# Later loads of the output weights, and two steps' attention weights transposed by DMA, in a thresholded attention with a SwiGLU layer behind it

## The chip, the cores and the metric

The kernel runs on one core of a Trainium2 chip. The metric is the device time of one execution in microseconds (us), here the median of 7 executions.

## The reference

The attention has 8 batches of 8 heads, 576 positions and a head width of 64. A row's weights are cut off below its maximum less `tau` (0.02). Its output, 4608 tokens of width 512, goes through an RMS norm and a gated layer of width 1536.

```python
scores = scale * np.matmul(q, k.transpose(0, 1, 3, 2))
thresh = np.max(scores, axis=-1, keepdims=True) - tau
scores = np.where(scores >= thresh, scores, -1000000000.0)
attn = np.exp(scores - np.max(scores, axis=-1, keepdims=True))
attn = attn / (np.sum(attn, axis=-1, keepdims=True) + 1e-09)
x = heads_joined(np.matmul(attn, v))               # 4608 x 512
xn = x / np.sqrt(np.mean(x * x, axis=-1, keepdims=True) + 1e-06) * rms_g
g = xn @ w_gate
out = (g * (1.0 / (1.0 + np.exp(-g))) * (xn @ w_val)) @ w_out
```

## The kernel before, in words

**Steps.** The work is cut into 144 score steps, counted from 0 in the code. A step is one pair of heads for one chunk of 128 query rows: 36 chunks by 4 head pairs. Each step goes through the same stations:

1. PE multiplies q by k in 32-bit floats into `s_ps` (line 697). I call this a burst, S. Until step 32 a burst is one step; after that, steps run together and are cut into bursts of 1024 columns (`CHOP`, line 1193).
2. DVE reads `s_ps`, scales it into one of three `ssb` buffers and finds the row extremes `mx` (line 730).
3. POOL makes the threshold `nth` from `mx` (line 771, some 0.2 us).
4. ACT applies the threshold, once for each head (line 782), and then the exponential into one of three 16-bit buffers `wsb` (line 789).
5. The weights of the step, 128 by 1152, are transposed into one of six `wt` buffers. There are two ways (lines 830 to 853). Either PE transposes nine blocks of 128 by 128 into PSUM (line 834; I call this T) and DVE copies them out in two pieces (line 843). Or SP issues one DMA transpose (line 849).
6. For two steps at a time PE multiplies `wt` by the values `va` (lines 870 and 875; I call this A), and DVE divides by the row sums (lines 892 and 893).

After four steps a chunk is complete: it is normed (ACT line 910, POOL lines 913 to 918) and transposed into `xnT`. Two or four chunks form a group of the gated layer. For each of its 12 blocks PE runs G (line 976, gate) and V (line 981, value), ACT a tanh (line 990), DVE two products (lines 993 and 998). Then O (line 1047, and line 1022 for the last group) multiplies by the output weights `wo`.

**Weights.** `w_gate` and `w_val` are loaded in twelve transfers through three staging buffers by SP (line 1125), and POOL scales and rounds them (line 1133). `wo` is loaded by four transfers of 384 KB that POOL issues (line 1145); no O can start before all four have landed.

**What sets the order.** All instructions are recorded as `Op` objects with an engine, an assumed cost, a priority and dependencies. `order_ops` (line 56) then plays a schedule with these assumed costs and writes each engine's instruction order out; the engines run in that fixed order. Where several operations of an engine could start at the same planned moment, the one with the smallest priority goes first. The priority is the step number plus an offset from the table `RANK` (line 26), looked up by the function that recorded the operation:

```python
        if o.prio >= 8.0 and o.eng != "SP":
            path = o.fn.__qualname__.split(".")
            o.prio += RANK.get(o.eng, {}).get((path[-3] if path[-3].startswith((
                "emit", "load", "setup", "transposed", "round")) else "main") + "/" + path[-1], 0.0)
```

A gated operation also waits for the burst of a certain step. The loads of `wo` are gated in this way (lines 1144 to 1147):

```python
        o = add("POOL", COST["pool_dma"], W_FROM + W_STEP * n + j + WO_AT, [], lambda o, j=j: nc.gpsimd.dma_start(
            out=wo[:, 3 * j:3 * j + 3], in_=wo_src[:, 3 * j:3 * j + 3]), dma=DMA_NS['wo'], bulk=True)
        wo_ld.append(gated(o, W_FROM + W_STEP * n + j + WO_AT))
```

With `W_FROM` 2.0, `W_STEP` 0.4 and n at 24 this is step 11 for the first load and step 14 for the last. The way of a step's transpose is chosen by this line:

```python
        if s < N_PE or s < N_ALT and s % 2:
```

Before, `N_PE` and `N_ALT` are both 16, so steps 0 to 15 go through PE and DVE and the other 128 through DMA.

Of the kernel before, what the change touches and what calls it, by code (L numbers as in the profile page):

```python
# [12 lines left out]

LAT = dict(PE=200.0, ACT=130.0, DVE=175.0, POOL=20.0, SP=0.0)
SELF = dict(PE=0.0, ACT=125.0, DVE=178.0, POOL=0.0, SP=0.0)
COST = dict(
# [7 lines left out]
SWITCH = 125.0  # L24

RANK = dict(
    ACT={"emit_ffn/ev": 450, "emit_ffn/store": 110, "emit_ffn/tanh": -300, "emit_k_tail/ev": -210, "emit_q_tail/ev": -80, "emit_qk/ev": 370,
        "emit_softmax/ex2": 60, "emit_softmax/prelu": 220, "emit_x/sq": -330},
    DVE={"emit_blocks/turn_k": 120, "emit_blocks/turn_kt": 288, "emit_blocks/turn_q": 293, "emit_burst/ttr": -57.4, "emit_ffn/ev": 320,
        "emit_ffn/gate": 60, "emit_ffn/silu": -59, "emit_k_tail/ev": 80, "emit_qk/ev": -20, "emit_softmax/ev": 320, "emit_x/ev": 50},  # L30
    PE={"emit_av/fn": -370, "emit_burst/fn": 16, "emit_ffn/gmm": 20, "emit_ffn/omm": 23, "emit_ffn/vmm": -40, "emit_k_tail/tr": 210, "emit_q_tail/tr":
        -160, "emit_qk/tr": 60, "emit_softmax/tr": -40, "emit_x/trp": 20},
    POOL={"emit_block_loads/swap": 40, "emit_softmax/nthr": -240, "emit_x/mean": -150, "emit_x/norm": -10, "round_/<lambda>": 130, "main/<lambda>":
        700, "main/cast": -280},
)


# [18 lines left out]
def order_ops(ops, ring_sizes):  # L56
# [26 lines left out]
    while len(out) < len(ops):  # L83
        best = None
        for e, lst in pending.items():
# [5 lines left out]
            for i in lst:  # L91
                o = ops[i]
                t = max(t0, ready_at[i])
                if o.ring is not None:
# [3 lines left out]
                    t = max(t, sorted(free)[o.nring - 1][0])  # L98
                other = e == "PE" and o.mode != mode
                t = max(t, o.release)  # L100
# [11 lines left out]
        cost = o.cost  # L112
        if e == "PE":
            if o.mode != mode:
# [35 lines left out]
def kernel(  # L150
# [98 lines left out]
    def gated(o, step):  # L249
        gates.append((o, step))  # L250
        return o

    def add(eng, cost, prio, deps, fn, **kw):
        o = Op(eng, cost, prio, deps, fn, **kw)
        ops.append(o)
        return o
# [30 lines left out]
    def setup():  # L287
        o_id = add("POOL", 2000.0, -100, [], lambda o: make_identity(nc, id32))

        def zero(o):  # L290
            nc.vector.memset(zcol, 0.0)
            nc.vector.memset(xn[0], 0.0)

        o_z = add("DVE", 350.0, -200, [], zero)

        def warm(o):

            for _ in range(WARM):
                nc.tensor.matmul(s_ps[0][:, 0:512], xn[0][:, 0:128], xn[0], start=True, stop=True)

        o_w = add("PE", WARM * 380.0, -200, [o_z], warm)

        def consts(o):
            nc.vector.tensor_copy(out=id16, in_=id32)
            nc.vector.memset(mhalf, -0.5)

        def vconst(o):
            for i in range(2):
                nc.vector.memset(va[i][:, :, :, D:D + 1], 1.0)
                nc.vector.memset(va[i][64:128, :, 8], 0.0)  # L310
                nc.vector.memset(va[i][0:64, :, 9], 0.0)

        o_c = add("DVE", 300.0, -100, [o_id, o_z], consts)
        o_v = add("DVE", 2000.0, -90, [], vconst)
        o_g = add("SP", 350.0, -0.5, [], lambda o: nc.sync.dma_start(
            out=rmsg, in_=moe_rms_g.rearrange("(c p) -> p c", p=128)), dma=100.0)
        return o_id, o_c, o_v, o_g
# [4 lines left out]
    def emit_qk(b, p, prio):  # L322
# [13 lines left out]
        def tr(o):  # L336
            for j in (1, 0):
                for c in range(4):
                    for r, rs in enumerate(HALF):
# [4 lines left out]

        t = gated(add("PE", COST["tr_qk"], -500.0, los + [o_id] + last_s.get(("k", b - 2, p), []), tr, ring="R",
                      nring=2, mode=1), prio)
        done = []
        for r, rs in enumerate(HALF):
            def ev(o, r=r, rs=rs):
                src = ring[t.slot[r]].rearrange("p (j c n) -> p j c n", j=2, n=64)  # L350
                if EVAC[r] == "ACT":
                    nc.scalar.copy(out=dst[:, :, :, rs], in_=src)
                else:
                    nc.vector.tensor_copy(out=dst[:, :, :, rs], in_=src)

            done.append(add(EVAC[r], COST["evac_qk" if EVAC[r] == "DVE" else "evac_qk_act"], prio, [t], ev, frees=(t, r)))
        for j in range(2):
# [7 lines left out]
    def emit_block_loads(b, g, base, prio):  # L365

        done = {}
        for j, src in ((1, k), (0, q)):
# [14 lines left out]
            for h in range(2):  # L383
# [4 lines left out]
                for dst, at in moves:  # L388
                    def swap(o, dst=dst, at=at):
                        nc.gpsimd.tensor_copy(out=dst, in_=at)  # L390

                    last = [add("POOL", COST["swap"], prio + SWAP_AT, last, swap)]
                spare_use.append(last[0])
# [28 lines left out]
    def emit_first():  # L422
# [13 lines left out]
        def load_k(p, prio):  # L436
# [6 lines left out]

            return add("SP" if p else "ACT", COST["sp_qk"], prio, before, load, dma=DMA_NS["qk"], bulk=True)

# [10 lines left out]
        def transposed(load, srcs, dsts, prio, engines):  # L456
# [9 lines left out]
            for e, (eng, lo, hi) in enumerate(engines):  # L466
                def ev(o, eng=eng, lo=lo, hi=hi):
                    copy = nc.scalar.copy if eng == "ACT" else nc.vector.tensor_copy
                    for i, m, dst in dsts:
                        if lo <= i < hi:  # L470
                            rs = slice(dst.base_partition(), dst.base_partition() + dst.shape[0])
                            copy(out=dst, in_=ring[t.slot[0]][rs, n * i:n * (i + m)].rearrange("p (a n) -> p a n", n=n))
# [13 lines left out]
        def emit_k(p, load, prio):  # L486
            nat = qkn[p % NQK]
            t, k_ready[p] = transposed(load, [pair(nat[:, 1, c]) for c in range(4)],
                                       [(0, 2, qkT[0][p][:, 0, 0:2]), (2, 2, qkT[0][p][:, 0, 2:4])], prio,
                                       [("ACT" if p in (1, 2) else "DVE", 0, 2), ("ACT", 2, 4)])  # L490
            tr_of[1].append(t)
# [84 lines left out]
    def emit_v(b, prio):  # L576
# [6 lines left out]
        def round_(dst, src):  # L583
            return lambda o: nc.gpsimd.tensor_scalar(out=dst, in0=src, scalar1=1.0, scalar2=1.0,
                                                     op0=ALU.mult, op1=ALU.mult)

        def free(p):
            return [o_v] + last_av.get((b - 2, p), [])

        for p in range(NP):  # L590
# [12 lines left out]
            if b >= BLOCKED and p == 0:  # L603
                lo = []
                for i in range(2 * V_PARTS):
# [8 lines left out]
                    lo[-1].lat = LAT_V  # L614
            ca = add("POOL", COST["cast_v"], (pr + V_CAST if b >= BLOCKED else pr + 1 if b else p - 1.0), (lo[2 * (p * V_PARTS // NP):][:2] if b >= BLOCKED else lo) + free(p), round_(
                t[:, p, 0:8, 0:D].rearrange("q (c h) d -> q h c d", h=2),
# [3 lines left out]
            if p == 0:  # L620
# [6 lines left out]
                for e in range(2):  # L627
                    es = slice(64 * e, 64 * e + 64)
                    ca = add("POOL", COST["cast_vt"], (pr + 1.3 if b else -0.5), [lt] + [x for p in range(NP) for x in free(p)],
                             round_(t[es, :, 8 + e, 0:D], vtl[es]))  # L630
# [135 lines left out]
    def emit_softmax(s):  # L766
# [62 lines left out]

        if s < N_PE or s < N_ALT and s % 2:  # L830
            def tr(o):
                for j in range(9):
                    r, c = divmod(j, 5)
                    nc.tensor.transpose(ring[o.slot[r]].bitcast(FP16)[:, 128 * c:128 * c + 128],
                                        wsb[s % NW].rearrange("p h s -> p (h s)")[:, 128 * j:128 * j + 128], id16)
# [308 lines left out]
    for j in range(4):  # L1144
# [4 lines that stand above are left out]
# [71 lines left out]
EPUSH = (0, 0.0)  # L1220
V_AFTER = (2, 0, 0, 0)
B1_BASE = 0.0
WO_AT = 0.0
BACKLOG = 3500.0
AV_PRIO = 2.5
HALF_PRIO = 1.2
# [16 lines left out]
W_STEP = 0.4  # L1243
N_XPE = 4
SOON = (0, 0.0)
N_PE = 16
N_ALT = 16
W_EVAC = ("DVE", "DVE")
EVAC = ("DVE", "ACT")
# [37 lines left out]
```

## Time and profile before

| | us |
|---|---|
| median of 7 executions (lowest, highest) | 534.26 (533.4, 535.13) |
| the profiled execution's own time | 536.02 |
| its span, first to last instruction | 534.2 |
| busy: PE, DVE, ACT, POOL | 523.3, 465.8, 443.8, 224.0 |
| PE transposes of weights, line 834 | 144 matmuls |
| their copies out of PSUM, line 843 | 32 copies, 7.7 + 6.7 |
| DMA transposes of weights, line 849 | 128 |
| loads of `wo`, first and last issue | 43.0, 61.2 |

The profile shows one execution. Its page gives busy time by engine and by group of instructions; other views give waits, stretches of time, the instructions in order of time, and the chain of work that ended last. A matmul's recorded time contains its way through the array, so the times of neighbours overlap; what one costs PE in a row of them is the distance from its start to the next start. The clock granted to PE was full from 40 us to 510 us in every stretch read.

### The profile page before, as it was taken

How to read it: one execution, taken by the hardware profiler on the slowest of the kernel's cores; microseconds unless marked ns; L12 is line 12 of the kernel's file. 1: busy time of each engine (PE TensorE's matmuls, PEld its weight loads, DVE VectorE, ACT ScalarE, POOL GpSimd, SP SyncE). 2: the span in 40 equal slices, each digit the busy share in tenths (PEclk: the TensorE clock that was granted, in tenths of full speed). 3: DMA queues.
4: the chain of work that ended last, by engine and by line, in shares of the span. 5: the costliest groups of instructions: out<-in, count | busy, mean ns of one | idle time of the engine just before them, and what ended most of it. 6: DMA issues, size and time to landing. Idle time of an engine off the chain costs nothing.

```text
span 534.2 us, 14401 instructions
## 1 busy us (share of the span) xinstructions
PE 523.3 (98%) x5368; PEld 276.2 (52%) x5368; DVE 465.8 (87%) x1348; ACT 443.8 (83%) x648; POOL 224.0 (42%) x478
## 2 busy tenths in 40 slices
PE   8899999999999999999999999999999999999996
PEld 4566676654545454545454444454545454454442
DVE  4789999979999799989997999999999898866641
ACT  5989999989997989899988898989999999962210
POOL 2268767334663155726742265735662111111000
PEclk9999999999999999999999999999999999999999
DMA  9999989989978797999979798999898778653013
GB/s 189 234 284 252 257 171 168 193 121 239 183 163 186 144 188 167 165 209 193 171 151 195 131 189 176 197 215 167 175 190 142 115 122 139 123 115 70 11 30 98
DMA packets 218887, 88.51 MB, mean 166 GB/s; under 512 B 195265, under 2 KB 204993, under 8 KB 218817
## 3 DMA queue, kind: packets, MB, share of 16 engines
q1 hardware_dynamic: 216016, 85.49, 80.4%
q0 software_dynamic: 1600, 1.57, 1.8%
q8 instruction: 42, 0.69, 0.5%
q10 hardware_dynamic: 1200, 0.52, 0.5%
q14 instruction: 29, 0.23, 0.1%
HBM read 37.75 MB, written 9.44 MB: 88 GB/s over the span
## 4 chain that ended last, share of the span: by engine, by line
PE 67%; DVE 12%; ACT 9%; DMA 4%; issue 4%; POOL 3%; SPq 0%; DVEq 0%; POOLq 0%; ACTq 0%
PE s_ps L697 21%; PE ring L1047 13%; PE ring L981 11%; PE ring L976 11%; DVE ssb L730 7%; ACT ssb L782 5%; PE ring L875 4%; ACT wsb L789 2%; PE s_ps L1022 2%; DMA wt<-wsb 2%; DVE sl L993 2%; ACT th L990 1%; PE ring L870 1%; DMA stg<-in_moe_w_val_dram 1%; PE s_ps L981 1%
## 5 line engine op out<-in xcount | busy, mean ns | idle before, releaser
L782 ACT ACTIVATE ssb<-ssb,nth 128x576 f32<-128x576 f32 x288 | 209.2, 766 | 21.3 <-POOL nth L771 20.6
L730 DVE CUSTOM_DVE_ANT_0 ssb<-s_ps,zcol 128x576 f32<-128x576 f32 (+8 forms) x288 | 169.5, 636 | 7.0 <-PE s_ps L697 4.4
L697 PE MATMUL s_ps<-qkt 64*64 64x288 f32 (+8 forms) x2256 | 171.4, 413 | 0.8 <-DVE mx L730 0.8
L789 ACT ACTIVATE wsb<-ssb 128x1152 f16<-128x1152 f32 x144 | 166.7, 1158 | 2.4 <-DMA wt<-wsb 0.3
L697 PEld LDWEIGHTS s_ps<-qkt 64*64 64x64 f32 x2256 | 82.4, 135 | 66.2 <-issue 28.6
L976 PE MATMUL ring<-xnT,wg 128*128 128x512 f16 (+1 forms) x464 | 109.2, 358 | 0.6 <-DVE sl L993 0.5
L981 PE MATMUL ring<-xnT,wv 128*128 128x512 f16 (+1 forms) x456 | 107.0, 357 | 0.5 <-DVE sl L993 0.2
L990 ACT ACTIVATE th<-ring 128x512 f32<-128x512 f32 (+1 forms) x116 | 62.5, 541 | 39.2 <-PE ring L976 38.9
L771 POOL TENSOR_SCALAR nth<-mx 128x2 f32<-128x2 f32 x144 | 30.8, 214 | 152.4 <-DVE mx L730 141.3
L993 DVE SCALAR_TENSOR_TENSOR sl<-th,ring 128x512 f32<-128x512 f32 (+1 forms) x116 | 72.0, 623 | 11.3 <-ACT th L990 11.1
L981 PEld LDWEIGHTS <-wv 128*128 128x128 f16 x480 | 44.5, 98 | 50.3 <-issue 11.1
L976 PEld LDWEIGHTS <-wg 128*128 128x128 f16 x480 | 42.9, 98 | 52.6 <-issue 15.1
L730 DVE CUSTOM_DVE_ANT_0 ssb<-s_ps,zcol,mxp 128x128 f32<-128x128 f32 (+7 forms) x112 | 52.9, 510 | 13.2 <-PE s_ps L697 13.0
L875 PE MATMUL ring<-va,wt 128*128 128x65 f16 (+1 forms) x1280 | 51.1, 193 | 0.0
L875 PEld LDWEIGHTS <-wt 128*128 128x128 f16 (+1 forms) x1280 | 46.1, 100 | 5.0 <-issue 0.6
L1047 PE MATMUL ring<-wo,hf 128*128 128x512 f16 x204 | 47.7, 380 | 0.0
L998 DVE TENSOR_TENSOR stg<-ring,sl 128x512 f16<-128x512 f32 (+1 forms) x57 | 35.5, 628 | 2.4
L998 DVE TENSOR_TENSOR hf<-ring,sl 128x512 f16<-128x512 f32 (+1 forms) x57 | 35.5, 627 | 1.8
L1047 PE MATMUL ring<-wo,stg 128*128 128x512 f16 x156 | 36.5, 380 | 0.0
L390 POOL COPY spare<-qkx 32x576 f32<-32x576 f32 x48 | 31.6, 658 | 7.3 <-DMA qkx<-in_k_dram 3.1
L893 DVE TENSOR_TENSOR xsb<-ring,rz 128x256 f32<-128x256 f32 x72 | 30.6, 425 | 3.5
L1047 PEld LDWEIGHTS <-hf 128*128 128x128 f16 x216 | 20.0, 98 | 25.9 <-issue 3.5
(75 smaller groups left out, 485.9 us busy)
## 6 DMA issues: line engine op xcount, KB each, us to landing
vst<-in_v_dram SPq DMA_DIRECT2D x32, 256.0 KB, 4.2
qkx<-in_k_dram SPq DMA_DIRECT2D x24, 288.0 KB, 3.4
qkx<-in_q_dram SPq DMA_DIRECT2D x24, 288.0 KB, 3.5
out_dram<-osb SPq DMA_DIRECT2D x48, 128.0 KB, 2.6
stg<-in_moe_w_gate_dram SPq DMA_DIRECT2D x6, 512.0 KB, 6.9
stg<-in_moe_w_val_dram SPq DMA_DIRECT2D x6, 512.0 KB, 6.6
wt<-wsb SPq DMA_TRANSPOSE x128, 3.6
out_dram<-osb SPq DMA_DIRECT2D x8, 256.0 KB, 3.0
```

Source lines behind the costliest of these rows:

```text
L390: nc.gpsimd.tensor_copy(out=dst, in_=at)
L697: nc.tensor.matmul(s_ps[h][rows, at:at + hi - lo], lhs(hs), k_of(bb, p, h)[hs, lo:hi], start=True, stop=True)
L730: nc.vector.tensor_tensor_reduce(out=ssb_of(s)[:, h, lo:hi], in0=s_ps[h][:, at:at + hi - lo], in1=zcol.to_broadcast([128, hi - lo]), scale ...
L782: nc.scalar.activation(out=sb_[:, h], in_=sb_[:, h], func=PRELU, scale=-1.0, bias=nth[m][:, h:h + 1], **PRELU_KW)
L789: nc.scalar.activation(out=wsb[s % NW], in_=sb_, func=AF.Exp)
L875: nc.tensor.matmul(ring[o.slot[0]][rs, at:at + D + 1], w[:, 5 * h + j, rs], va[vi][:, p, 2 * j + h], start=False, stop=(h == 1 and j == 3))
L976: nc.tensor.matmul(ring[o.slot[0]][:, 0:n], wg[d][:, fs], xnT[slot][:, d, 0:n], start=(d == 0), stop=(d == 3))
L981: nc.tensor.matmul(ring[o.slot[0]][:, 0:n], wv[d][:, fs], xnT[slot][:, d, 0:n], start=(d == 0), stop=(d == 3))
L990: nc.scalar.activation(out=th[i][:, 0:n], in_=ring[g.slot[0]][:, 0:n], func=AF.Tanh, scale=0.5)
L993: nc.vector.scalar_tensor_tensor(out=sl[i][:, 0:n], in0=th[i][:, 0:n], scalar=1.0, in1=ring[g.slot[0]][:, 0:n], op0=ALU.add, op1=ALU.mult)
L998: nc.vector.tensor_tensor(out=hf[hi][:, 0:n], in0=ring[vv.slot[0]][:, 0:n], in1=sl[i][:, 0:n], op=ALU.mult)
L1047: nc.tensor.matmul(ring[(first or o).slot[0]], hf[hs[fc][0]][:, 128 * j:128 * (j + 1)], wo[:, fc], start=(fc == 0), stop=(fc == NFC - 1))
```

## The change

Three settings differ. `WO_AT` goes from 0 to 6, which gates the four loads of `wo` on steps 17 to 20. `N_PE` goes from 16 to 12 while `N_ALT` stays at 16, so that of steps 12 to 15 only the odd ones, 13 and 15, keep the PE transpose; steps 12 and 14 (the thirteenth and fifteenth when counted from one) get a DMA transpose. And most offsets in `RANK` have new values, with two functions (`emit_av/half` and `emit_ffn/ev_half`) newly in it.

```diff
 RANK = dict(
-    ACT={"emit_ffn/ev": 450, "emit_ffn/store": 110, "emit_ffn/tanh": -300, "emit_k_tail/ev": -210, "emit_q_tail/ev": -80, "emit_qk/ev": 370,
-        "emit_softmax/ex2": 60, "emit_softmax/prelu": 220, "emit_x/sq": -330},
-    DVE={"emit_blocks/turn_k": 120, "emit_blocks/turn_kt": 288, "emit_blocks/turn_q": 293, "emit_burst/ttr": -57.4, "emit_ffn/ev": 320,
-        "emit_ffn/gate": 60, "emit_ffn/silu": -59, "emit_k_tail/ev": 80, "emit_qk/ev": -20, "emit_softmax/ev": 320, "emit_x/ev": 50},
-    PE={"emit_av/fn": -370, "emit_burst/fn": 16, "emit_ffn/gmm": 20, "emit_ffn/omm": 23, "emit_ffn/vmm": -40, "emit_k_tail/tr": 210, "emit_q_tail/tr":
-        -160, "emit_qk/tr": 60, "emit_softmax/tr": -40, "emit_x/trp": 20},
-    POOL={"emit_block_loads/swap": 40, "emit_softmax/nthr": -240, "emit_x/mean": -150, "emit_x/norm": -10, "round_/<lambda>": 130, "main/<lambda>":
-        700, "main/cast": -280},
+    ACT={"emit_ffn/ev": 510, "emit_ffn/store": -10, "emit_ffn/tanh": -320, "emit_k_tail/ev": -260, "emit_q_tail/ev": -80, "emit_qk/ev": 500,
+        "emit_softmax/ex2": 120, "emit_softmax/prelu": 220, "emit_x/sq": -250},
+    DVE={"emit_av/half": 30, "emit_blocks/turn_k": 70, "emit_blocks/turn_kt": 280, "emit_blocks/turn_q": 290, "emit_burst/ttr": -70, "emit_ffn/ev":
+        350, "emit_ffn/ev_half": -50, "emit_ffn/gate": -20, "emit_ffn/silu": -40, "emit_k_tail/ev": 40, "emit_qk/ev": -20, "emit_softmax/ev": 300,
+        "emit_x/ev": 20},
+    PE={"emit_av/fn": -310, "emit_burst/fn": 30, "emit_ffn/gmm": 34, "emit_ffn/omm": 45, "emit_ffn/vmm": -30, "emit_k_tail/tr": 290, "emit_q_tail/tr":
+        -140, "emit_qk/tr": 50, "emit_softmax/tr": -20, "emit_x/trp": -80},
+    POOL={"emit_block_loads/swap": 50, "emit_softmax/nthr": -270, "emit_x/mean": -90, "emit_x/norm": -30, "round_/<lambda>": 150, "main/<lambda>":
+        740, "main/cast": -190},
 )
...
-WO_AT = 0.0
+WO_AT = 6.0
...
-N_PE = 16
+N_PE = 12
 N_ALT = 16
```

The new file has one line more in `RANK`, so its later line numbers are one higher. Since the order is planned anew from these numbers, the order of instructions differs on every engine: the work itself, apart from the two transposes, is the same.

## Prediction

> **What bounds the kernel now.** I read the page first, for who is busy, then the busy time of five stretches, cut where step 12 starts (45.9 us), step 20 (67.3), after step 32 (120), at step 80 (263.5) and at the last step (467.3).
>
> ```profile
> PE 523.3 (98%) x5368; PEld 276.2 (52%) x5368; DVE 465.8 (87%) x1348; ACT 443.8 (83%) x648; POOL 224.0 (42%) x478
> ```
>
> ```profile
> 45.90:67.30 21.40, 21.40 (x303) 14.87 (x302) 21.11 (x61) 20.41 (x32) 16.18 (x30) 1.00 1.08 270
> 67.30:120.00 52.70, 52.52 (x657) 33.62 (x656) 48.35 (x145) 50.39 (x81) 28.38 (x59) 1.00 0.93 164
> 120.00:263.50 143.50, 142.63 (x1499) 71.24 (x1498) 137.36 (x415) 131.86 (x187) 73.77 (x154) 1.00 0.93 185
> 263.50:467.30 203.80, 203.07 (x2153) 100.81 (x2152) 190.10 (x577) 186.64 (x264) 81.90 (x182) 1.00 0.86 160
> 467.30:534.20 66.90, 61.87 (x332) 28.75 (x330) 35.80 (x60) 18.60 (x32) 3.30 (x8) 0.99 0.30 65
> ```
>
> The columns are the stretch, its length, busy PE, weight loads, DVE, ACT and POOL, the clock, the DMA share and GB/s. PE's 98% says little, because neighbouring matmuls overlap in the records. Two timeline rows show the real price:
>
> ```profile
> 68.09 1.20 PE L697 MATMUL s_ps<-qkt 64*64 64x288 f32 x16
> 69.23 0.61 PE L976 MATMUL ring<-xnT,wg 128*128 128x256 f16 x4
> 69.67 0.60 PE L981 MATMUL ring<-xnT,wv 128*128 128x256 f16 x4
> ```
>
> G's four matmuls are followed by V after 0.44 us, not 0.61: 0.11 us for 256 columns, so 0.216 for 512. The burst takes 1.14 to the next start, of which some 0.96 is the rhythm of its matmuls; about 0.18 is lost on leaving 32-bit work. With such distances PE's pure work is 474 us. In the first stretches it leaves clear gaps: about 10 of 13.4 us is used at 40 to 67 us. From 93 us on, work and the fixed loss at each burst fill the time; the waits view of 250 to 470 us agrees, its largest waits of PE are "issue", which nobody can shorten:
>
> ```profile
> PEld s_ps L697 <- issue: 16.5, 69, 0.4
> ...
> DVE ssb L730 <- PE s_ps L697: 7.1, 12, 1.2
> ```
>
> So PE sets the pace from step 20 or so to the end. Between steps 12 and 20, where the change sits, DVE has 0.3 us free in 21.4, ACT 1.0, and PE waits for them. There I followed the chain of work:
>
> ```profile
> 56.15 0.20 POOL nth L771
> ...
> 56.41 0.83 POOL wo L1145
> 57.24 0.04 issue
> 57.28 1.35 POOL wg L1133 x2
> ...
> 61.26 0.81 POOL wo L1145
> ...
> 62.12 1.37 POOL wv L1133 x2
> 63.49 0.73 DVE ssb L730
> ```
>
> For 7 us this chain runs through POOL, and two of the issues of `wo` are links of it.
>
> **The two transposes.** PE loses 18 matmuls. One T occupies it from 54.38 to 54.90 us, so 2 x 0.52 = 1.04 us. DVE loses four copies:
>
> ```profile
> L843 DVE COPY wt<-ring 128x640 f16<-128x640 f16 x16 | 7.7, 483 | 1.6 <-PE ring L834 1.6
> ...
> L843 DVE COPY wt<-ring 128x512 f16<-128x512 f16 x16 | 6.7, 416 | 0.0
> ```
>
> That is 2 x (0.483 + 0.416) = 1.80 us. SP gains two issues, median 1.31 us each; it is idle in most of 55 to 63 us. They go between loads: the first ahead of the last load of `w_val` and a load of `v`, the second between two loads of the k block of batch 2. These wait behind it for the exponential of step 12 (ends at 52.5 us) and of 14 (57.9). The k block is first used by step 36, some 117 us, and its swaps start at 65 us, so about 4 us of delay is hidden; uncovered it would cost those 4 us.
>
> What is unknown is the landing. The 128 transposes of before take 3.2 to 5.5 us (median 3.6), but the first is issued at 63.7. Loads issued between 43 and 57 us, where DMA is full (share 1.00, 266 GB/s), take 6.3 to 8.9; one of `w_val` issued at 53.2 takes 6.5. So a landing costs 3.2 to 8.9 us. I take 4.5: two of the four loads of `wo`, issued at 43.0 and 49.9, leave this stretch, 768 KB or 3 us of transfer at 266 GB/s. In the changed order A of steps 12 and 13 stands one burst earlier than before, behind S of step 16, which ends at 57.3 us on the old clock. From 52.5 plus 4.5 the weights are there at 57.0. At the fast end nothing waits, at the slow end A waits 4.1 us.
>
> A row and a rule differ here. Nine blocks land together in 3.6 us. The Trainium skill ("VectorE: DVE Perf Modes", The three transpose paths and the rules behind it) gives 390 ns for a 128 by 128 block on TensorE and 1309 ns by DMA, and recommends TensorE where PSUM is an acceptable target, which speaks against this change. Nine blocks in turn would be 11.8 us by that page, an estimate, and A would then wait 7 us.
>
> **The loads of wo.** The four issues (0.86 us of POOL each) move from between casts of 43 to 61 us to places behind the thresholds of steps 16, 17, 20 and 21. Two issues leave the chain above, 0.83 + 0.81 = 1.64 us. They delay later thresholds, at 65 to 75 us, where POOL had waited for DVE; behind each stands one threshold, so uncovered they cost ACT up to 0.86 each. The first O moves from behind S 27 to behind S 31, some 104 us; the last load issued near 75 lands by 84 at the slowest 8.9. No wait from this.
>
> **The order.** I compared the built orders. The bursts are 95 in both. PE changes from one kind of matmul to another 481 times before and 469 times after; a change costs 0.01 (G to V) to 0.18 us (S to anything), and added up by kind this is 0.7 us less; since kinds with few samples are in it, I take 0.5. From bursts 43 to 59 (steps 52 to 80) the fillings are the same. Behind step 80 the new order puts less of the gated layer between bursts: after the last score it has 308 of its matmuls left, against 284. These 24 x 0.216 = 5.2 us move into the tail, where PE works alone. If PE sets the pace before, that costs nothing: the last score comes 5.2 us earlier.
>
> **The sum.** At steps 12 to 20 the chain offers 1.64 us, DVE 1.80 + 0.29 idle, PE 1.04. ACT's work does not change, so what can come through there is ACT's idle time, 1.0 us. The order gives 0.5 more on PE. Forecast: -1.5. The profiled execution took 536.02 us, 1.76 over the median, with its span at 534.2; both would lose the same 1.5. From the median of 534.26 this makes **532.8 us**. Its own range is 530.8 (chain and DVE both come through: 1.64 + 1.80 = 3.4) to 533.2.
>
> **The rivals.**
>
> *Nothing comes through* (534.3, from 533.2 to 535.3). ACT is idle for 1.0 us in 21.4 there, and what PE saves turns into its waits. For: three engines are full in the first stretch. Against: the chain there runs through POOL, not ACT.
>
> *DVE sets the end of the attention* (536.8). The 24 matmuls moved to the tail cost 5.2 us there. DVE sheds only the gated layer's products that go with them, 2.7 us by the rows in both orders. If DVE's pace decides from step 80 on, the last score comes 2.7 us earlier and not 5.2, so this costs 2.5. For: DVE is 93% busy from 263.5 us on. Against: its 13.7 us of idle time there, and the waits above, where DVE waits for PE. It decides if DVE has almost no idle time left between steps 80 and 143.
>
> *A meets weights that have not landed* (535.7 to 537). With 6.5 us, the weights of step 12 arrive at 59.0 and PE waits 1.7; the same again at 14 makes 3.4, less the 1.5. For: every load of that stretch. Against: the two loads of `wo` that left it.
>
> *The words cover only a part*: the offsets in `RANK` reorder every engine. This has no price of its own; its effects are in the terms above.
>
> **Chances.** Forecast 0.48, nothing 0.22, DVE 0.18, late weights 0.12. A measurement of this kernel can tell some 0.2%, 1.1 us, from no change. So faster 0.48, same 0.22, slower 0.30. The range is from 530.8 to 536.8, where the slower rivals lie.
>
> **What would show it.** Right: 126 matmuls at line 834 and 28 copies at line 843; no wait of A for `wt` near 57 and 63 us; step 20 starting about 1 us earlier; the last score about 6 us earlier and the tail 5 us longer; DMA landings at 50 to 57 us below 6 us. Wrong: A or the weight load ahead of it idle for `wt<-wsb` by over 1 us; bursts waiting for DVE's extremes behind step 80; thresholds queued behind `wo` at 65 to 75 us with ACT idle; step 20 no earlier.

## The result, and the profile after

The changed kernel takes **538.95 us** (median; 536.11 to 543.53) against 534.16 (532.45 to 535.34) for the kernel before in the same runs: a ratio of 1.0094 (95% interval 1.0075 to 1.0113). It is slower by 4.8 us, and the prediction, 532.8 with a range up to 536.8, was wrong in sign. The executions of the changed kernel scatter more than those before, and with the clock: the seven with a mean granted clock of 0.997 or more have a median of 537.65 us, the five below it 540.14, while of the 96 executions of the kernel before that ran beside the experiments six were below it. So some 1.3 of the 4.8 us go with stretches of lower clock.

The profiled execution took 538.81 us with a span of 537.0. The page's line of busy times says nothing of the loss, except that PE is busy 1 us less in a longer span:

```profile
PE 522.3 (97%) x5350; PEld 275.9 (51%) x5350; DVE 464.1 (86%) x1344; ACT 443.4 (83%) x648; POOL 224.2 (42%) x478
```

The same five stretches as before, with the same cuts (columns as above: stretch, length, busy PE, weight loads, DVE, ACT, POOL, clock, DMA share, GB/s):

```profile
45.90:67.30 21.40, 20.71 (x276) 13.72 (x274) 19.96 (x59) 21.30 (x35) 14.99 (x28) 1.00 0.87 196
67.30:120.00 52.70, 50.70 (x637) 32.49 (x637) 47.42 (x142) 48.34 (x78) 29.10 (x60) 1.00 1.12 188
120.00:263.50 143.50, 142.72 (x1498) 70.94 (x1499) 136.17 (x410) 131.38 (x187) 73.86 (x154) 1.00 0.97 185
263.50:467.30 203.80, 202.47 (x2170) 102.02 (x2161) 190.45 (x582) 189.19 (x267) 82.64 (x184) 1.00 0.88 162
467.30:537.00 69.70, 64.16 (x328) 29.49 (x326) 35.69 (x56) 16.77 (x29) 2.87 (x6) 0.98 0.27 60
```

The DMA share fell from 1.08 to 0.87 in the first stretch and rose from 0.93 to 1.12 in the second, because `wo` went from the one to the other. In the second PE has 2 us without work, where before it had 0.2.

Cuts by time mix different work in the two kernels, so the accounts below are made by **steps**: the time from DVE's first read of the scores of one step to its first read of those of another, taken from the trace. Start to step 12 is left out of the reasoning: it differs by 3 us from one profile to the next among kernels with the same matmuls there (43.1 us in e3, 44.0 in e5, 45.9 before). The two longest of the old order, before and e10 (45.6), are the two in which the clock granted to PE fell to 0.50 there, from 24.1 to 27.5 us. By an estimate 3.4 us at half the clock lose at most 1.7 us, most of the 1.8 by which the profile of before stands above its median. The profile after has such a stretch too, from 25.1 to 28.5 us. From step 12 until the last 4 us both profiles ran at full clock.

| steps, us | 12 to 20 | 20 to 52 | 52 to 80 | 80 to 143 | 143 to end |
|---|---|---|---|---|---|
| before | 23.6 | 102.5 | 91.5 | 203.8 | 66.9 |
| after | 24.0 | 104.4 | 91.4 | 200.3 | 72.3 |
| difference | +0.4 | +1.9 | -0.1 | -3.5 | +5.4 |

Two things stand out, +1.9 us at steps 20 to 52, and a tail that gained 5.4 us while the attention ahead of it gave back only 3.5: another 1.9. All five differences come to 4.1 of the 4.8 us. To judge them: where kernels do the same work in the same order, the order of before repeats a stretch within 0.5 us, but the new order repeats steps 12 to 20 only within 1.0 (25.1 in e7, 24.1 in e9) and steps 80 to 143 within 1.3 (199.3 in e13, 200.6 in e7). So the +0.4 is not clear of this scatter.

**The first loss** is a wait for transposed weights. The waits of 60 to 95 us in the profile after (engine and line, what it waits for: us in total, times, longest), then PE's row in time, then the piece of the chain of waits there:

```profile
PEld L871 <- DMA wt<-wsb: 2.1, 1, 2.1
...
PE ring L871 <- DMA wt<-wsb: 2.0, 1, 2.0
```

```profile
80.04 0.23 PE L871 MATMUL ring<-va,wt 128*128 128x130 f16 x1 [2.00 <-DMA wt<-wsb]
```

```profile
72.51 7.49 DMA wt<-wsb
```

A, whose line is now 871, stands idle for 2 us until a transpose that took 7.5 us to land. The DMA issues of 60 to 90 us show the same for all transposes there, before and after (count, median us from issue to landing):

```profile
wt<-wsb SPq DMA_TRANSPOSE x9, 3.6
```

```profile
wo<-in_moe_w_out_dram POOLq DMA_DIRECT2D x4, 384.0 KB, 7.2
...
wt<-wsb SPq DMA_TRANSPOSE x9, 6.3
```

**The second loss** has no big wait. It is many small ones of the weight load ahead of a burst, for DVE's extremes. The waits of the weight loads from 263 to 470 us, before and then after:

```profile
PEld s_ps L697 <- issue: 15.3, 64, 0.4
PEld s_ps L697 <- DVE mxp L730: 3.4, 8, 0.5
```

```profile
PEld s_ps L698 <- issue: 12.7, 55, 0.4
PEld s_ps L698 <- DVE mxp L731: 7.9, 18, 0.7
```

Before, a burst waited 8 times for DVE there, after 18 times. Weight loads run beside PE's matmuls (97% and 51% of the span in the busy line above), so these 7.9 us are not the loss itself. The distances from start to start of PE's matmuls in the traces give it: over steps 80 to 143 the 35 bursts, each with the distance from the matmul ahead of it, take 63.9 us before and 65.5 after, 1.6 more.

### The profile page after: what moved, and what is told of

It reads as the page before. It is cut to its first block, busy times and chain, and to the rows that moved or that the text cites. A ratio compares the mean times of both kernels' runs of the same rounds, so it can differ in the third digit from the quotient of the medians.

```text
span 537.0 us, 14371 instructions
## 1 busy us (share of the span) xinstructions
PE 522.3 (97%) x5350; PEld 275.9 (51%) x5350; DVE 464.1 (86%) x1344; ACT 443.4 (83%) x648; POOL 224.2 (42%) x478
## 4 chain that ended last, share of the span: by engine, by line
PE 56%; DVE 19%; ACT 9%; DMA 5%; POOL 4%; issue 4%; SPq 1%; DVEq 0%; POOLq 0%; ACTq 0%
PE s_ps L698 16%; PE ring L1048 11%; DVE ssb L731 10%; PE ring L982 10%; PE ring L977 9%; ACT ssb L783 5%; DMA wt<-wsb 3%; PE ring L876 3%; ACT wsb L790 3%; DVE sl L994 2%; PE s_ps L1023 2%; DMA vst<-in_v_dram 2%; PE s_ps L1048 1%; ACT th L991 1%; DVE hf L999 1%
## 5 line engine op out<-in xcount | busy, mean ns | idle before, releaser
L698 PEld LDWEIGHTS s_ps<-qkt 64*64 64x64 f32 x2256 | 83.5, 134 | 67.0 <-issue 26.9
L977 PE MATMUL ring<-xnT,wg 128*128 128x512 f16 (+1 forms) x452 | 106.1, 357 | 0.4 <-DVE sl L994 0.4
L991 ACT ACTIVATE th<-ring 128x512 f32<-128x512 f32 (+1 forms) x113 | 60.9, 540 | 26.8 <-PE ring L977 26.4
L994 DVE SCALAR_TENSOR_TENSOR sl<-th,ring 128x512 f32<-128x512 f32 (+1 forms) x113 | 70.2, 623 | 6.9 <-ACT th L991 6.9
L914 POOL TENSOR_SCALAR irm<-ssq 128x1 f32<-128x1 f32 x36 | 6.9, 191 | 67.5 <-ACT xn L911 67.0
L871 PE MATMUL ring<-va,wt 128*128 128x130 f16 (+1 forms) x158 | 31.9, 225 | 2.9 <-DMA wt<-wsb 2.9
L1048 PE MATMUL ring<-wo,stg 128*128 128x512 f16 x144 | 33.4, 379 | 0.0
```

The costliest lines, as they stand in the source:

```text
L698: nc.tensor.matmul(s_ps[h][rows, at:at + hi - lo], lhs(hs), k_of(bb, p, h)[hs, lo:hi], start=True, stop=True)
L871: nc.tensor.matmul(ring[o.slot[0]][rs, at:at + 2 * (D + 1)], w[:, 4, rs], va[vi][:, p, 8:10].rearrange("p e d -> p (e d)"), start=True, st ...
L977: nc.tensor.matmul(ring[o.slot[0]][:, 0:n], wg[d][:, fs], xnT[slot][:, d, 0:n], start=(d == 0), stop=(d == 3))
L991: nc.scalar.activation(out=th[i][:, 0:n], in_=ring[g.slot[0]][:, 0:n], func=AF.Tanh, scale=0.5)
L994: nc.vector.scalar_tensor_tensor(out=sl[i][:, 0:n], in0=th[i][:, 0:n], scalar=1.0, in1=ring[g.slot[0]][:, 0:n], op0=ALU.add, op1=ALU.mult)
L1048: nc.tensor.matmul(ring[(first or o).slot[0]], hf[hs[fc][0]][:, 128 * j:128 * (j + 1)], wo[:, fc], start=(fc == 0), stop=(fc == NFC - 1))
```

## The experiments

Four theories were set against each other. **W**: the late loads of `wo` share the DMA with the transposes of steps 16 to 23 and hold them up by their bytes. **O**: the new order is slower by itself, since it puts 24 matmuls of the gated layer behind the last score and leaves the attention to DVE's pace. **T**: the two new transposes of steps 12 and 14 cost time. **P**: POOL's four issues of `wo`, which now stand ahead of thresholds, cost time. Where a kernel is called "order frozen", the planner's order is kept and only the named instructions are moved or replaced. Line numbers of all experiments are those of the kernel before. Each ran beside the kernel before (533.99 to 534.34 in these runs).

**e1, the changed kernel with `wo` early.** The four loads are put back ahead of the thresholds of steps 11, 13, 16 and 17, order otherwise frozen:

```diff
+    seq = [o for o in seq if o not in wo_ld]
+    for o, s in zip(wo_ld, WO_BEFORE_NTH):
+        seq.insert(seq.index(nth_op[s]), o)
+WO_BEFORE_NTH = (11, 13, 16, 17)
```

> The changed kernel with its whole order kept, only the four loads of wo put back ahead of the thresholds of steps 11, 13, 16 and 17 on POOL, as before the change. Theory W (the late loads of wo crowd the DMA transposes of steps 16 to 23): the wait of A of 2.0 us near 80 us goes, transposes land in 3 to 5 us again, and the median falls from 538.95 to 532.5 to 534.5 us. Theory O (the new order costs, with its 24 matmuls moved to the tail and DVE setting the pace): stays at 537.5 to 539.5. Theory T (the transposes of steps 12 and 14): now these two land later among the loads of wo, so above 539.

Measured 540.23, ratio 1.0112 (1.0087 to 1.0137). Steps 20 to 52 fell to 102.2 us, as W wants, but steps 12 to 20 rose from 24.0 to 29.5. The transpose of step 12 now took 6.8 us to land (3.3 in the changed kernel), and A waited 0.9 us for it. Most of the rise lies elsewhere: ACT waited 4.7 us for thresholds, and the chain of waits ahead of the longer of these two waits (2.9 us) runs through a load of `v` that SP issues behind that transpose:

```profile
54.75 6.08 DMA vst<-in_v_dram
...
60.90 0.62 POOL va L584
...
62.20 0.80 POOL wo L1145
...
63.07 0.23 POOL nth L771
```

POOL waited 3.1 us for this load, with an issue of `wo` and the threshold behind it. PE then waited 1.65 us for DVE, and from 67.8 to 71.2 us its granted clock was 0.50: a burst took 2.87 us there, which takes 1.20 at full clock. So W's number missed and T's was met, but not by the transposes alone: without the loads beside them they land in time (below). In the new order the early place of `wo` collides with what SP moves there, the two new transposes among it, and part of the loss is the clock.

**e2, the kernel before with `wo` late.** The same edit in the order of before, frozen, with `WO_BEFORE_NTH = (17, 18, 21, 22)`:

> The kernel before with its whole order kept, only the four loads of wo moved behind, ahead of the thresholds of steps 17, 18, 21 and 22 on POOL, as in the changed kernel. Theory W: slower by 2.5 to 5 us (536.7 to 539.2), with a wait of A or of ACT for a transpose between 70 and 85 us. Theory O: no change or up to 1 us faster (533.2 to 534.5). Theory T: no change.

Measured 539.65, ratio 1.0089 (1.0070 to 1.0108). The late loads alone make a loss of the size of the whole change's. The waits of 65 to 95 us, and the landings of all its transposes (before: at most 5.5):

```profile
PEld L870 <- DMA wt<-wsb: 5.2, 4, 2.0
PE ring L870 <- DMA wt<-wsb: 4.3, 3, 1.8
...
ACT wsb L789 <- DMA wt<-wsb: 2.6, 1, 2.6
```

```profile
DMA to landing us min/median/max: 3.2/3.6/11.5
```

Three transposes in a row took 11.5, 9.6 and 9.9 us. PE waits for `wt`, and ACT waits too, because `wsb` comes free only when its transpose has read it. Steps 20 to 52 take 108.7 us against 102.5 before, and nothing else changes.

**e3, the kernel before with the two transposes.** Order frozen; at the place of T of steps 12 and 14 SP issues the DMA transpose, and the nine matmuls and two copies are left out:

```diff
+        by_dma = s in BY_DMA and (lambda: nc.sync.dma_start_transpose(out=wt[s % NWT], ...))
-                for j in range(9):
+                for j in range(0 if by_dma and [by_dma()] else 9):
...
-                    eng.tensor_copy(out=wt[s % NWT][:, lo:hi], ...)
+                    by_dma or eng.tensor_copy(out=wt[s % NWT][:, lo:hi], ...)
+BY_DMA = (12, 14)
```

> The kernel before with its whole order kept, only the nine PE transposes and two copies of steps 12 and 14 taken out and one DMA transpose each put at their place in the recorded order. Theory W: 533.2 to 534.5, these two are not the cause. Theory T: slower by over 1.5 us, with A waiting for wt near 60 us, since wo is still loaded in that stretch. Theory O: no change.

Measured 534.86, ratio 1.0014 (1.0001 to 1.0027): PE has 1.04 us and DVE 1.80 us less to do, and the time does not fall. Steps 12 to 20 take 23.5 us against 23.6. ACT's busy time by group over these steps tells why; the last figure is its idle time, with what ended it:

```profile
L352 ACT COPY qkt<-ring 128x512 f32<-128x512 f32 x1 | 0.6, 585 | 0.8 <-PE ring L341 0.8
```

```profile
L352 ACT COPY qkt<-ring 128x512 f32<-128x512 f32 x1 | 0.6, 586 | 0.8 <-PE ring L341 0.8
```

The first row is the kernel before, the second e3. ACT's one real idle time before is a wait for a transpose of k by PE, and the change takes nothing from it; in e3 another 0.5 us stands ahead of ACT's exponentials, 0.3 of it for a transpose by DMA. That ACT sets the pace of these steps is argued from its idle time, not tested by taking work from it.

**e4, the kernel before with both** (the edits of e2 and e3):

> The kernel before with its whole order kept and both moves of the change, the loads of wo behind and steps 12 and 14 by DMA, that is the change without its new offsets in RANK. Theory W: 536.5 to 539, like the move of wo alone, perhaps 1 us less. Theory O: 533 to 534.5, the rest of the loss comes with the offsets. Theory T: like the transposes alone.

Measured 540.21, ratio 1.0116 (1.0097 to 1.0135). The two parts do not help each other: it is e2 with some 0.6 more.

**e5, e6 and e7: small loads of `wo`.** Each load brings 16 of 512 columns, the rest of `wo` is set to zero by POOL at the start. The issues stay where they were, and the bytes go. e5 is the kernel before, e6 is e2, e7 the changed kernel.

```diff
-            out=wo[:, 3 * j:3 * j + 3], in_=wo_src[:, 3 * j:3 * j + 3])
+            out=wo[:, 3 * j:3 * j + 3, 0:16], in_=wo_src[:, 3 * j:3 * j + 3, 0:16])
```

> The kernel before with each load of wo cut to 16 of 512 columns and the rest of wo set to zero by POOL at the start, so most of the output weights are left out; order and issue of the four loads stay. Theory W (bytes of wo crowd other transfers): landings at 45 to 62 us shorten by 2 to 3 us, the time falls by 0 to 1.5 us (532.6 to 534.1), since nothing on the path waits for a transfer there. Theory P (the issues on POOL ahead of thresholds cost, not the bytes): 534.1, no change.

> The same small loads of wo (most of the output weights left out), but issued late, ahead of the thresholds of steps 17, 18, 21 and 22 as in the second experiment, which took 539.65 us. Theory W: transposes of steps 16 to 21 land in 3 to 5 us, no wait of A, and the time is that of the early small loads within 1 us (532.5 to 534.5). Theory P: stays above 538.

> The changed kernel with small loads of wo (most of the output weights left out) in its own order. What is left over the early small loads on the order before is the price of the new order with the two DMA transposes. Theory W alone: 532 to 533.5, with my forecast's gain. Theory O (24 matmuls moved into the tail at DVE's pace): 1 to 2.5 us over the small early loads, so 534.5 to 536.

Measured: e5 534.5 (ratio 1.0007, 0.9996 to 1.0018), e6 533.9 (0.9995, 0.9984 to 1.0006), e7 536.46 (1.0037, 1.0023 to 1.0052). Three things follow. At their old place the bytes of `wo` cost nothing (e5). At the late place of e2 the whole loss, 539.65 - 533.9 = 5.75 us, is bytes; the issues of POOL, which are all still there, cost nothing in this order, so P falls. And the changed kernel loses 2.5 us by the bytes (medians; steps 20 to 52 fall by 2.2, to 102.2 us, and none of e7's seven executions had a low clock) and keeps a loss of 2.2 us (536.46 against 534.22) without them: that is left for O.

**e8, the new offsets alone** (`RANK` of the changed kernel, `WO_AT` and `N_PE` as before, planned anew; 304 matmuls of the gated layer behind the last score):

> The kernel before with the new offsets in RANK alone, planned anew: loads of wo and PE transposes as before. Theory O: slower by 1 to 2.5 us (535 to 536.6), since this order also leaves 4 us of the gated layer more to the tail. Theory W: within 0.8 us of 534.1, because wo is loaded early and 16 steps go through PE.

Measured 537.27, ratio 1.0054 (1.0038 to 1.0070). A new order without a late load or a new transpose can lose 3 us. By steps its tail gains 4.4 us and the stretches ahead of it give back 2.0; whether DVE's pace is the reason here too was not tested.

**e9 and e10: less work for DVE.** With the small loads, DVE's two products of the gated layer work on the first half of their columns in the groups from chunk 12 on; every engine's order stays. e9 is e7, and e10 is e5, with this cut:

```diff
+        hn = 64 * len(parts) if parts[0][0] >= 12 else 128 * len(parts)
-                    out=sl[i][:, 0:n], in0=th[i][:, 0:n], scalar=1.0, in1=ring[g.slot[0]][:, 0:n],
+                    out=sl[i][:, 0:hn], in0=th[i][:, 0:hn], scalar=1.0, in1=ring[g.slot[0]][:, 0:hn],
-                nc.vector.tensor_tensor(out=hf[hi][:, 0:n], in0=ring[vv.slot[0]][:, 0:n], in1=sl[i][:, 0:n], op=ALU.mult)
+                nc.vector.tensor_tensor(out=hf[hi][:, 0:hn], in0=ring[vv.slot[0]][:, 0:hn], in1=sl[i][:, 0:hn], op=ALU.mult)
```

> The changed kernel with the small loads of wo (16 of 512 columns, the rest zeros), and with the silu and the gate of DVE cut to the first half of their columns in the gated groups from chunk 12 on (about step 55 to the end; 144 DVE instructions of 0.6 us become about 0.3 us, the second halves stay unfilled); the order of every engine is that of the changed kernel with small loads (536.46). Read beside the same cut in the kernel before. O, in the form that DVE's pace makes the new order slow from step 55 on: the difference to the kernel before with the same cut falls from 2.0 to 0.8 us or less. O, in the form that the new order loses in steps 20 to 52, or at TensorE's own switches, and DVE has no part in it: the difference stays at 1.6 us or more. Both say that the time itself falls below 536.0; if it does not, DVE has no part in the pace after step 55 at all.

> The kernel before with the small loads of wo (534.5) and the same cut of DVE's silu and gate to half their columns in the gated groups from chunk 12 on. O with DVE's pace in the new order alone: gains less than 1 us (533.5 or more), for the old order hardly waits for DVE. If DVE paces both orders, it gains as much as the changed kernel does (2 us or more).

Measured 533.22 (ratio 0.9983, 0.9971 to 0.9994) and 532.67 (0.9971, 0.9957 to 0.9985). The difference of the two orders falls from 2.0 us to 0.55, as O with DVE's pace has it. e10 gained 1.8 us, between the two numbers expected of it: the old order gains from a lighter DVE too, but not behind step 80 (its profile has 0.8 us of the gain in steps 52 to 80 and the rest in no stretch). Steps 80 to 143 show it best. DVE's cut is the same in both, 34 us over the kernel; the old order stays at 203.9 us (203.8 before), the new one falls from 200.6 in e7 to 198.4. The waits of the weight loads, 263 to 470 us, in e9:

```profile
PEld s_ps L697 <- issue: 15.0, 66, 0.4
...
PEld s_ps L697 <- DVE mxp L730: 1.7, 4, 0.4
```

The 18 waits for DVE's extremes (7.9 us in e7, as in the changed kernel) have become 4, and the 35 bursts of steps 80 to 143 with the distances ahead of them take 63.9 us again, as before, against 65.5 in the changed kernel.

**e11, e2 in twelve pieces.** The order of before with `wo` late, but as twelve loads of 128 KB, one ahead of each threshold of steps 13 to 24:

```diff
+    for fc_, st_ in enumerate(WO_BEFORE_NTH):
+        o = copy.copy(wo_ld[0])
+        o.fn = lambda o, i=fc_: nc.gpsimd.dma_start(out=wo[:, i:i + 1], in_=wo_src[:, i:i + 1])
+        seq.insert(seq.index(nth_op[st_]), o)
+WO_BEFORE_NTH = (13, 14, 15, 16, 17, 18, 19, 20, 21, 22, 23, 24)
```

> The order of before, frozen, with wo loaded late in twelve loads of 128 KB instead of four of 384 KB: one ahead of each threshold of steps 13 to 24, so that the same bytes come over the same stretch (about 46 to 81 us) without a lump. W as a lump (a transpose that is issued beside a 384 KB load waits for most of it): the largest landing of a transpose falls from 11.5 to 7 us or less, and the time from 539.65 to 535.5 or less. W as a sum of bytes (wo, the staged weights and the transposes together are too much for those 35 us, however cut): 537.5 or more. P (twelve issues of POOL at 0.86 us ahead of thresholds instead of four): more than 540.

Measured 534.93, ratio 1.0015 (0.9997 to 1.0033), where e2 had 539.65. The largest landing falls from 11.5 to 7.3 us, a little over the 7 expected. So it is the lump more than the sum: 1.5 MB issued within 16 us (61.2 to 77.6) cost 5.5 us, the same 1.5 MB over 34 us (47.9 to 82.0) cost 0.6 by the medians, with an interval that reaches to 1.8, and 1.3 in steps 20 to 52. Whether the size of one load or the distance between them matters was not told apart, and four of the twelve pieces are issued ahead of the first DMA transpose (62.0 us), so a third of the bytes has left its neighbourhood as well.

**e12, the words without the offsets** (`WO_AT` 6 and `N_PE` 12 with the `RANK` of before, planned anew, small loads; 270 matmuls behind the last score):

> The changed kernel's late wo and its two transposes by DMA, with the ordering offsets of before, planned anew, and the small loads of wo (so that no bytes crowd the transposes). 270 matmuls of the gated layer are left for the tail, against 284 before and 308 after. O by the offsets (the new offsets make the order that loses 2 us): 533.5 to 535.0, at the level of before. The rival, that any order planned with the two DMA transposes and the late loads loses what the changed kernel loses, whatever the offsets: 536.0 or more.

Measured 539.63, ratio 1.0093 (1.0068 to 1.0118). This refutes the form of O that blames the new offsets alone. With the old offsets the two settings lose 5.1 us (e12 against e5) with hardly a byte of `wo`, at steps 20 to 52 (106.2 us) and 52 to 80 (96.0). In the first of these PE waits 2.7 us for DVE's extremes with no gated matmul at that place, and then its granted clock is 0.50 for 3.4 us. The burst behind the wait, and the busy columns of the 3.4 us (the last but two is the clock):

```profile
122.68 3.65 PE L697 MATMUL s_ps<-qkt 64*64 64x384 f32 x32 [2.73 <-DVE mxp L730]
```

```profile
123.30:126.70 3.40, 3.40 (x39) 2.60 (x32) 0.24 (x1) 3.27 (x4) 0.00 (x0) 0.50 1.11 274
```

A burst of 32 matmuls took 1.96 us at full clock ten microseconds earlier, so the low clock is part of these 5.1 us (three of the six executions had one). What is lost in steps 52 to 80 was not followed. The new offsets repair most of that, down to the 2.0 of e7. Each table fits the settings that it stands with.

**e13, the changed kernel with `wo` in twelve pieces** (the edit of e11):

> The changed kernel, order frozen, with wo in twelve loads of 128 KB, one ahead of each threshold of steps 13 to 24, in place of its four loads of 384 KB. W as a lump, in the changed kernel too: the 2 us by which TensorE waits for a transposed tile near 80 us shrink to about 1 or less, and the time comes down from 538.95 to that of the changed kernel with small loads (536.46), within 0.8: 535.9 to 537.3. If what the small loads took away in the changed kernel was the sum of bytes, it stays at 538.3 or more.

Measured 537.47, ratio 1.0056 (1.0037 to 1.0074): just outside the range expected, and well below 538.3. Steps 20 to 52 fall from 104.4 to 102.2 us, the value without the bytes, and A waits for no transpose between 60 and 95 us. But steps 12 to 20 take 25.6 us against 24.0. The first pieces stand beside the transposes of steps 12 and 14 there, which land in 5.2 and 4.4 us (3.3 and 3.2 before the pieces); no wait for them shows, and e7, with hardly any bytes, takes 25.1 us as well, where e9 with the same work takes 24.1, so about 1 us of this is scatter and the rest is open. The wait near 80 us goes with the lump in the changed kernel too. How much time that is worth is less clear, since steps 12 to 52 together fall by 0.6 us only (128.4 to 127.8).

**e14, the changed kernel with the cut of DVE's work** (the edit of e9, full loads of `wo`):

> The changed kernel with its own four loads of wo, and DVE's silu and gate cut to the first half of their columns in the gated groups from chunk 12 on (the second halves stay unfilled). If the two causes (lumps of wo beside the transposes, and DVE's pace in the new order) lie at different times and add up, it gains what the same cut gained with the small loads, 536.46 to 533.22, so 535.0 to 536.4. If the time lost to the lumps is what DVE's pace would have cost anyway (one cause seen twice), it falls to 534.2 or less.

Measured 535.45, ratio 1.0028 (1.0004 to 1.0052), as expected of two losses that add up. Steps 80 to 143 take 198.5 us as in e9; steps 20 to 52 take 105.6, with A's wait still there. That is 1.2 us more than in the changed kernel, for nearly the same work. In this execution the granted clock was 0.50 from 81.0 to 84.4 us, behind that wait, and a burst took 2.19 us where it takes 1.20 at full clock:

```profile
79.74 0.23 PE L870 MATMUL ring<-va,wt 128*128 128x130 f16 x1 [2.11 <-DMA wt<-wsb]
...
81.02 2.19 PE L697 MATMUL s_ps<-qkt 64*64 64x288 f32 x16
```

**e15, moving DVE's work instead of leaving it out.** In the kernel before, order frozen, eleven evictions of outputs (line 1062) are done by ACT:

```diff
-            def ev(o, oi=oi, mo=mo, at=at, on_dve=on_dve, cols=...
+            def ev(o, oi=oi, mo=mo, at=at, on_dve=on_dve and (streamed or ci < 12 or j % 2 == 0), cols=...
```

> The kernel before, order frozen, with eleven evictions of the gated layer's outputs (0.6 us of DVE each, groups from chunk 12 on) done by ACT in the same place; nothing is left out. O with DVE's pace: cutting some 43 us of DVE's work there brought the kernel before 1.8 us, so 6.6 us bring 0.3 us, if ACT (92% busy there, 5 us more) does not take the pace: 533.7 to 534.3. If ACT takes the pace: 535 or more.

Measured 534.14, ratio 0.9994 (0.9979 to 1.0009): no difference that can be measured. (The 43 us in the expectation are 34 by the pages.) None of the kernels that do the whole work is faster than the kernel before.

## Why the prediction was wrong

**The two transposes: priced right, worth nothing.** The work went as counted. Line 835 has 126 matmuls, and the copies fell from 7.7 + 6.7 us to

```profile
L844 DVE COPY wt<-ring 128x640 f16<-128x640 f16 x14 | 6.8, 484 | 1.0 <-PE ring L835 1.0
...
L844 DVE COPY wt<-ring 128x512 f16<-128x512 f16 x14 | 5.8, 415 | 0.0
```

which is 1.8 us less. The two new transposes landed in 3.3 and 3.2 us, faster than the 4.5 taken. No A waits near 57 or 63 us; these rows of the timeline show no idle time ahead of it:

```profile
56.80 0.22 PE L871 MATMUL ring<-va,wt 128*128 128x130 f16 x1
...
62.77 0.22 PE L871 MATMUL ring<-va,wt 128*128 128x130 f16 x1
```

So the rival "A meets weights that have not landed" did not happen where it was placed. It happened 20 us later, to the transposes that were there already.

What failed is "what can come through there is ACT's idle time, 1.0 us". Steps 12 to 20 take 24.0 us, not 22.6. The 1.0 was a ceiling, and I took it as the value without asking what ACT waits for. It waited 0.8 us for a transpose of k (line 341), which no part of the change touches; in the changed kernel that wait is gone and another of 0.9 us, for thresholds, stands in its place. With nothing taken from ACT's chain, 1.64 us of POOL, 1.80 of DVE and 1.04 of PE saved beside it are worth nothing: steps 12 to 20 take 23.6 us before, 23.5 in e3 and 23.5 in e4, where the loads are late as well.

**The loads of wo: "No wait from this" was the first failed step.** I asked when the loads land against the first O, and what POOL's issues do to thresholds. Both answers hold (e6). I did not ask what the loads do to the transfers at their new place, though the row was in my hands: loads issued at 43 to 57 us, where `wo` was, took 6.3 to 8.9 us. The crowding moved with `wo`, from a stretch in which steps transpose on PE to one in which every step waits for a DMA transpose. In the changed kernel it costs 1.9 us by steps and 2.5 us by the medians of e7. The Trainium skill ("DMA: Bandwidth & Descriptors", Issuing engines are not separate DMA queues) says that transfers issued by different engines share the same 16 DMA engines and interleave. The rows agree: `wo` is issued by POOL, the transposes by SP, and the one stretched the other from 3.6 to 11.5 us (e2). Weighed against the late loads, this rule would have put a price where I put none.

**The order: "If PE sets the pace before, that costs nothing" was the second.** The tail gained 5.4 us, as counted (5.2). The last score came 3.5 us earlier in steps 80 to 143, not 5.2. DVE shed 190.10 - 186.92 = 3.2 us in these steps and kept its idle time (13.7 us before, 13.3 after), so the stretch shrank by what DVE shed, not by what PE shed. That is the rival "DVE sets the end of the attention", with 1.9 us for the 2.5 it named. With DVE's work cut, the stretch takes the 198.4 and 198.5 us of e9 and e14: 5.4 less than before, all that the tail had gained.

The busy columns over steps 80 to 143, after and then in e9 (each row's times are that kernel's own steps 80 and 143):

```profile
264.50:464.70 200.20, 198.87 (x2146) 100.66 (x2145) 186.92 (x571) 185.74 (x263) 81.31 (x181) 1.00 0.88 161
```

```profile
260.60:459.00 198.40, 197.45 (x2146) 97.26 (x2147) 167.77 (x572) 185.37 (x263) 81.58 (x181) 1.00 0.89 164
```

I had given that rival 0.18 because of DVE's 13.7 us of idle time, and had written that it decides "if DVE has almost no idle time left". This condition was wrong. DVE's idle time is spread over small waits of the chain from scores to extremes and back (the waits above), and it stayed at 13.3 us when PE had less to put between the bursts. The old order is at the edge: PE sets its pace there (e10 leaves the stretch at 203.9), and taking 5.2 us from PE alone crosses over to DVE.

**The sum.** Forecast: -1.0 at steps 12 to 20, -0.5 from the order, nothing for the rest. By steps: +0.4, +1.9 (lump of `wo`), -0.1, -3.5 + 5.4 = +1.9 (DVE's pace): 4.1 of the 4.8 us; the rest is in no stretch of the two profiles, and the clock has a part in it by the executions. The 0.5 us from fewer changes of kind on PE is not seen in any stretch; that DVE's pace hides it is likely, not shown. The range failed because it held the rivals as alternatives, up to 536.8, while two losses of different stretches add up.

**What stays open.** e9 still stands 0.55 us above e10, and its steps 12 to 20 take 24.1 us against 23.6. These steps differ by 1.6 us among the kernels with the new order and late loads (24.0 to 25.6); 1.0 of it also lies between e7 and e9, which do the same work there. Why the clock falls in more of the changed kernel's executions (5 of 12; none of 7 in e7, none of 12 in e9) was not tested: that A's wait for late weights brings it about fits e14, but the changed kernel's profile shows the same wait at full clock. Which of the settings makes the planner lose so much with the old offsets (e12) was not tried.

## What to carry to other kernels

When a transfer is moved to hide it, ask not only when it lands and who issues it, but which transfers of its new neighbourhood sit on the path; a bulk load beside a transpose that every step waits for can cost time on the path (5.5 us in e2, 1.9 by steps in the changed kernel), and if it must be there, try it in pieces that are spread out. A ceiling (an engine's idle time) is not a gain until the trace shows what that engine waits for and that the change removes it. Moving work of one engine behind a stretch shortened that stretch here by what the next engine shed, so compare the two sheds, not the idle shares; and add up the rivals that lie in different stretches.

## What the runs showed of the hardware

A DMA transpose of one step's weights, 128 by 1152, lands in 3.2 us when little runs beside it (before, 70.1 to 73.3 us), and in 11.5, 9.6 and 9.9 us between loads of 384 KB issued by another engine (e2). The same bytes in pieces of 128 KB, issued over 34 us instead of 16, stretched it to 7.3 us at most (e11). I had not expected that the DMA share does not tell the two apart. The stretch of 60 to 80 us in e2, then in e11:

```profile
60.00:80.00 20.00, 17.00 (x214) 11.72 (x213) 16.54 (x50) 17.15 (x29) 14.51 (x26) 1.00 1.07 142
```

```profile
60.00:80.00 20.00, 19.59 (x249) 13.70 (x251) 18.77 (x57) 19.54 (x33) 16.22 (x33) 1.00 1.04 158
```

The share is 1.07 and 1.04, and PE is busy for 17.0 and 19.6 of the 20 us. Whether a transfer on the path is late is read from its landing times, not from the share.

The clock granted to PE fell to 0.50 behind waits of PE: after a wait of 1.65 us in e1, 2.73 in e12 and 2.11 in e14, for 3.4 us each, and during one of 3.41 in e4, for 6.8 us. It stayed full after the wait of 2.00 us in the profile of the changed kernel, and after those of 1.75 and 1.25 in e2, so the length of the wait alone does not decide it.
